# Written order of issue carried into the second product of an attention and channel-mixer kernel

## The chip, the core and the metric

One core of a Trainium2 chip runs the kernel. The metric is the device time of one execution in microseconds (us). The core has a matmul engine (PE, with its weight loads as PEld), a vector engine (DVE), a scalar engine (ACT), a general engine (POOL) and an engine that issues most transfers (SP). Each has its own queue of instructions, worked off in order; semaphores tie them together.

## The reference

Attention with a decay per head, in blocks, gives x of shape (4, 768, 512). A low-rank mixer along the sequence and a channel mixer of two products follow:

```python
xt = x.transpose(0, 2, 1)
h = xt @ U @ V
u = x + h.transpose(0, 2, 1)
ch = np.maximum(u @ w_ch1, 0.0) @ w_ch2
return (u + ch).astype(np.float32)
```

`u` has 3072 rows of 512 numbers, `w_ch1` is 512 x 2048, `w_ch2` is 2048 x 512.

## The kernel before

All products are made at fp32 accuracy from numbers split in three: high, low, and a third part that corrects both. One full product of two tiles is then two "high" matmuls (high and low of one operand) on one PSUM bank and one "third" matmul on another, or on the same bank once ACT has scaled it (`raise_high`, L966).

The first product, r = u @ w_ch1, is cut in `g`, six groups of 512 rows of u, and `ft`, 16 blocks of 128 columns of w_ch1. Groups 0 to 3 are plain (`hidden`, `single`); groups 4 and 5 come last and use seven products in place of eight for most pairs of blocks: `seven_of` (L1213) for j = 1 to 7, `eight_of` (L1264) for j = 0. These products take sums of parts of u, the **forms** (a11, a12, s1 to s4 and so on), made by `form` (L1103): a `high` on ACT (L1109), `rest` (L1112) and `last` (L1115) on DVE, each 128 x 1024. Each r tile (128 x 512) goes to memory (`r_d`).

The order of this part is written by hand, inside `tc.manual_schedule()` (`ordered`, L811 to L1409). `sequence` (L1070) lists its 53 products; `tick()` (L1173) is called once in each of them, between its high matmuls and what follows, and runs the steps that `strew` (L1045) has put at that number: loads and splits of weights, forms, stores. A tick is some 1.4 us, in j = 0 some 2.7 us. The last pair, j = 7, ends with `(7, 3)`, `(7, 6)` on the running banks z and d, and `(7, 7)` on the same two. `taken` (L1198) copies a bank to an r tile on ACT (L1200), `add_to` (L1195) adds another on DVE (L1196), `give` (L1203) stores the tile two ticks later, or at once when fewer than two are left.

The second product, ch = relu(r) @ w_ch2, runs over 96 steps (g, ft), ft within g. A step loads an r tile (`fetch`, L1302, three buffers), takes its relu and splits it into m (`split`, L1307: L1311 on ACT, L1312 and L1313 on DVE; four buffers) and makes four pieces of three matmuls (`product`, L1318: L1327, L1329, L1331). `ahead(i)` (L1360) loads step i + 3 and splits step i + 2. A piece has two PSUM banks for the 16 steps of its group; pieces 0 and 1 of group 0 take tags b1 and b2, pieces 2 and 3 take a1 and a2. After step 15 of a group `finish` (L1341) adds u, loaded by `residual` (L1333, L1339), and stores.

The 16 blocks of w_ch2 are split in three as well (`w2_split`, L1369, by `divided_steps`, L255). Five (`EARLY`) are done in ticks of the first product. The other eleven are divided in the loop of the second: in step i the load of block i + 5 (L1381), then L266 on ACT, L267 and L270 on DVE. Their places are those of the forms, which the first product no longer needs.

From L1409 on, the order in which instructions are put in the queues is chosen by the planner of the language: it goes by its own costs, and puts an instruction that it finds ready in front of written ones that it finds waiting. The first steps of the second product are thus mixed into the end of the first.

```python
    ordered.close()
    spare = 1
    STAG = 3
    for i in range(len(steps) - STAG):
        g, ft = steps[i]
        ahead(i)
        if i + EARLY < FT:
            for step in w2_split(i + EARLY):
                step()
```

Of the kernel before, what the change touches and what calls it, by code (L numbers as in the profile page):

```python
# [9 lines left out]
F32R = mybir.dt.float32r  # L10
# [4 lines left out]
P = 128  # L15
# [3 lines left out]
def kernel(  # L19
# [28 lines left out]
    nc = tc.nc  # L48
# [4 lines left out]
    C = H * D  # L53
    CT = C // P
    FF = moe_w_ch1.shape[1]
    FT = FF // P
# [6 lines left out]
    TG = N // P  # L63
# [10 lines left out]
    hl_pool = ctx.enter_context(tc.tile_pool(name="hl", bufs=FG))  # L74
    d_pool = ctx.enter_context(tc.tile_pool(name="d", bufs=FG))
# [28 lines left out]
    w2_d = [dram.tile([P, C], FP32, name=f"w2_d{ft}") for ft in range(FT)]  # L104
    forms_d = [dram.tile([P, 8, C // 2], FP32, name=f"forms_d{j}") for j in range(FT // 2)]

    def tmp(name):
        return wconv.tile([P, C], FP32, tag="tmp", bufs=2, name=name)
# [100 lines left out]
    def plain(keep, key, tag="wf"):  # L209

        def dst():
            if key not in keep:
                keep[key] = (
                    tmp("wg") if tag == "tmp" else
                    plain_pool[-1].tile(
                        [P, C], FP32, tag=tag, bufs=1 if len(plain_pool) == 1 else 3, name="wf"
                    )
                )
            return keep[key]

        return dst
# [33 lines left out]
    def divided_steps(parts, fetch, engine, apart=False, raw=None):  # L255

        st = {}

        def load():
            st["w"] = raw() if raw and apart else plain({}, 0)()  # L260
            fetch(st["w"])

        def split():
            hi, low, third = parts()
            w = st["w"][:, 0 : hi.shape[-1]]
            nc.scalar.mul(hi, w, E * NEAR)  # L266
            nc.vector.scalar_tensor_tensor(  # L267
                low, hi.bitcast(FP32), -1.0 / E, w, ALU.mult, ALU.add
            )
            engine.tensor_tensor(  # L270
                out=third, in0=low.bitcast(FP32), in1=hi.bitcast(FP32), op=ALU.subtract
            )

        def high():
            st["hi"], st["low"], st["third"] = parts()
            nc.scalar.mul(st["hi"], st["w"][:, 0 : st["hi"].shape[-1]], E * NEAR)

        def low():
            nc.vector.scalar_tensor_tensor(  # L279
                st["low"], st["hi"].bitcast(FP32), -1.0 / E,  # L280
                st["w"][:, 0 : st["hi"].shape[-1]], ALU.mult, ALU.add,
            )

        def third():
            engine.tensor_tensor(  # L285
                out=st["third"], in0=st["low"].bitcast(FP32), in1=st["hi"].bitcast(FP32),
                op=ALU.subtract,
            )

        return [load, high, low, third] if apart else [load, split]  # L290

    more_w = []
# [31 lines left out]
    raw = {}  # L324

    def parts(s):
        return 2 if s == 0 else 1
# [65 lines left out]
    st = {}  # L393
# [305 lines left out]
    for s in range(NS):  # L699
# [6 lines left out]
        step = [("fade", s)] * (c > 0)  # L706
# [104 lines left out]
    ordered = ctx.enter_context(ExitStack())  # L811
# [55 lines left out]
    def banks(n, other):  # L867

        tags = ("b1", "b2") if other else ("a1", "a2")
        pzs, pds = ([bank([P, N], name, tag) for i in range(n)] for name, tag in zip(("pz", "pd"), tags))  # L870
        return list(zip(pzs, pds))
# [56 lines left out]
    places = (0, 5), (1, 8), (1, 9), (1, 20), (1, 21), (1, 23), (2, 7), (2, 8)  # L928
# [19 lines left out]
    LAST, EARLY = FT - 4, 5  # L948
# [96 lines left out]
    def strew(units, steps):  # L1045
        assert len(units) == len(steps)
        for n, step in zip(units, steps):
            at.setdefault(n, []).append((units[0], step))
# [21 lines left out]
    sequence = []  # L1070
# [10 lines left out]
    for n in range(0, len(sequence), 2):  # L1081
# [6 lines left out]
        def fetch(w, n=n):  # L1088
            for i, (j, form) in enumerate(sequence[n : n + 2]):
                nc.sync.dma_start(out=w[:, i * HC : (i + 1) * HC], in_=forms_d[j][:, form])  # L1090
# [5 lines left out]
    places, form_of = {}, {}  # L1096

    def place(n):
        hl = hl_pool.tile([P, 2, CT, N], F32R, tag="hl", name="s_hl")
        d = d_pool.tile([P, CT, N], F32R, tag="d", name="s_d")  # L1100
        places[n] = [(hl[:, :, c : c + 2], d[:, c : c + 2]) for c in range(0, CT, 2)]

    def form(key, n, i, of):  # L1103

        hl, d = form_of[key] = places[n][i]
        hi, low = hl[:, 0], hl[:, 1]

        def high():
            nc.scalar.mul(hi, of, NEAR)  # L1109

        def rest():
            nc.vector.tensor_tensor(out=low, in0=of, in1=hi.bitcast(FP32), op=ALU.subtract)  # L1112

        def last():
            nc.vector.scalar_tensor_tensor(  # L1115
                d, hi.bitcast(FP32), E, low.bitcast(FP32), ALU.mult, ALU.subtract
            )

        return [high, rest, last]

    def sums(out, a, b, op=ALU.subtract):
        return [lambda: nc.vector.tensor_tensor(out=out, in0=a, in1=b, op=op)]

    g0, g1 = range(FG, NG)
    a11, a12, a21, a22 = (whole[g][:, c : c + 2] for g in (g0, g1) for c in (0, 2))
    s12 = sums_pool.tile([P, 2, 2, N], FP32, tag="s", bufs=1, name="s")
    s1, s2 = s12[:, 0], s12[:, 1]
    s3 = s12[:, 0]
# [31 lines left out]
    def last_forms():  # L1160
        place(3)
        strew((0,), sums(s3, a11, a21))
        strew((0, 1, 1), form("s4", 3, 0, a12))
        strew((1, 2, 2), form("s3", 3, 1, s3))
        strew((3,), [forms_made])

    def forms_made():
        whole_ctx.close()
# [29 lines left out]
    def taken(acc, scale):  # L1198
        t = r_pool.tile([P, N], FP32, tag="r", name="r")
        nc.scalar.mul(t, acc, scale)  # L1200
        return t

    def give(t, ft, g):  # L1203
        n = at["now"] + 2
        step = lambda: nc.sync.dma_start(out=r_d[ft][g], in_=t)
        strew((n,), [step]) if n < len(sequence) else step()

    def both(z, d):
        t = taken(z, 4096.0 + 1.0)
# [89 lines left out]
    steps = [(g, ft) for g in range(NG) for ft in range(FT)]  # L1299
    rs, ms = {}, {}  # L1300
# [6 lines left out]
    def split(i):  # L1307
        r = rs.pop(i)
        ms[i] = m = m_pool.tile([P, 3, N], F32R, tag="m", name="m")
        hi, low = m[:, 0].bitcast(FP32), m[:, 1].bitcast(FP32)  # L1310
        nc.scalar.activation(out=m[:, 0], in_=r, func=AF.Relu, scale=NEAR)  # L1311
        nc.vector.scalar_tensor_tensor(m[:, 1], r, 0.0, hi, ALU.max, ALU.subtract)  # L1312
        nc.vector.scalar_tensor_tensor(m[:, 2], hi, E, low, ALU.mult, ALU.subtract)  # L1313
# [4 lines left out]
    def product(i, n, parts=range(3)):  # L1318
        g, ft = steps[i]
        m, (hi, low, third) = ms[i], w2t[ft]  # L1320
        if ft == 0:
            acc[n] = banks(1, n // 2 != spare)[0]
        pz, pd = acc[n]
        cols = slice(n * P, (n + 1) * P)
        first, end = ft == 0, ft == FT - 1
        if 0 in parts:
            nc.tensor.matmul(out=pz, lhsT=m[:, 0, cols], rhs=hi, start=first, stop=False)  # L1327
        if 1 in parts:
            nc.tensor.matmul(out=pz, lhsT=m[:, 1, cols], rhs=low, start=False, stop=end)  # L1329
        if 2 in parts:  # L1330
            nc.tensor.matmul(out=pd, lhsT=m[:, 2, cols], rhs=third, start=first, stop=end)  # L1331
# [28 lines left out]
    def ahead(i):  # L1360
        if i + 3 < len(steps):
            fetch(i + 3)
        if i + 2 < len(steps):
            split(i + 2)


    w2t = {}

    def w2_split(ft):  # L1369
        def raw():  # L1370
            t = e_pool[0].tile([P, 3, C], F32R, tag="e", name="w2")
            w2t[ft] = [t[:, i, :] for i in range(3)]
            return w2t[ft][2].bitcast(FP32)

        if ft >= EARLY and (ft - EARLY) % 4 == 0:
            hl = hl_pool.tile([P, 4, 2, C], F32R, tag="hl", name="w2_hl")
            d = d_pool.tile([P, 4, C], F32R, tag="d", name="w2_d")
            for i in range(min(4, FT - ft)):
                w2t[ft + i] = [hl[:, i, 0], hl[:, i, 1], d[:, i]]
        return divided_steps(  # L1380
            lambda: w2t[ft], lambda w: nc.sync.dma_start(out=w, in_=w2_d[ft]),  # L1381
            nc.gpsimd if ft < EARLY else nc.vector,
            ft < EARLY, raw,
        )

    def begin_second():
# [7 lines left out]
    total = len(sequence)  # L1394
    strew((total - 14,), [begin_second])
    for ft in range(EARLY):
        n = 6 + 7 * ft
# [2 lines left out]
        strew((total - 9 + n,), [lambda n=n: fetch(n)])  # L1400
    for n in range(2):
        strew((total - 4 + 2 * n,), [lambda n=n: split(n)])
    pending = []
    for j in range(FT // 2):
        (seven_of if j in SEVEN else eight_of)(j, pending)
    for end in pending:
        end()
    assert list(at) == ["now"]
    ordered.close()  # L1409
    spare = 1  # L1410

    STAG = 3
    for i in range(len(steps) - STAG):
        g, ft = steps[i]
        ahead(i)
        if i + EARLY < FT:
            for step in w2_split(i + EARLY):
                step()
        if i == len(steps) - STAG - 1:
            ahead(i + 1)  # L1420
        if ft == FT - STAG - 1:
            residual(g)
        for n in range(TG):
            product(i, n)
        del ms[i]
        if ft == FT - 1:
            for n in range(TG):
                finish(g, n)
# [36 lines left out]
```

## Time and profile before

| what | value |
|---|---|
| three runs | 643.47, 643.88 (median), 645.03 us |
| the profiled execution | 643.46 us, of it a span of 641.6 us from the first to the last instruction |
| PE busy | 632.1 us, 99% of the span |
| DVE, ACT, POOL busy | 464.5, 331.9, 147.8 us |
| mean granted PE clock | 0.996 of full speed |
| matmuls from 300 to 350, 350 to 400 us | 220, 204 |
| last matmul of the first product starts | between 377.0 and 377.6 us |

In a row of the timeline the columns are start, duration, engine, line, operation, tiles written and read, how often; where several are merged, the duration runs from the first start to the last end. A bracket is idle time of that engine before the row, with what ended it. "Matmuls are pipelined": the end of one lies after the start of the next. In a table by stage each row is a stretch, with the busy time of each engine and the count of its instructions, then the granted clock, the share of the transfer engines and GB/s.

### The profile page before, as it was taken

What the parts mean: (1) busy time and instruction counts of PE and PEld (TensorE: products, weight loads), DVE (VectorE), ACT (ScalarE), POOL (GpSimd) and SP (SyncE); (2) the same over time, 40 slices, a digit from 0 to 9 for tenths busy, and PEclk for the clock granted to TensorE, in tenths of its full rate; (3) what the DMA queues carried; (4) which work ended last, traced back from release to release, by engine and by line L of the source; (5) the groups of instructions that cost most, each with busy time, mean ns of one, the idle gap of its engine ahead of it and who ended that gap; (6) DMA issues with size and microseconds to landing.
All of it is one profiled execution on the core that took longest, in us unless ns stands there. A gap on an engine that the chain in (4) does not pass through costs nothing.

```text
span 641.6 us, 13618 instructions
## 1 busy us (share of the span) xinstructions
PE 632.1 (99%) x5200; PEld 530.3 (83%) x5200; DVE 464.5 (72%) x738; ACT 331.9 (52%) x607; POOL 147.8 (23%) x124
## 2 busy tenths in 40 slices
PE   8999999999999999999999999999999999999997
PEld 7988989788888888887887768888888888888886
DVE  6765878657878889779698899685575755855854
ACT  4775865646777777777776644232322322323320
POOL 4475978000000000000567600030120300300300
PEclk9999999999999999999999989999999999999999
DMA  9989995458987888665667786362363363543521
GB/s 234 254 202 256 256 231 146 139 192 289 317 300 276 285 307 287 222 203 176 211 214 229 253 314 219 97 228 101 98 230 98 116 202 100 174 147 99 181 83 65
DMA packets 141379, 128.83 MB, mean 201 GB/s; under 512 B 82498, under 2 KB 99394, under 8 KB 141314
## 3 DMA queue, kind: packets, MB, share of 16 engines
q1 hardware_dynamic: 116192, 121.53, 59.0%
q10 hardware_dynamic: 25122, 6.42, 4.4%
q8 instruction: 41, 0.67, 0.4%
q14 instruction: 24, 0.20, 0.1%
HBM read 78.64 MB, written 48.89 MB: 199 GB/s over the span
## 4 chain that ended last, share of the span: by engine, by line
PE 94%; ACT 2%; DMA 2%; SPq 1%; issue 1%; DVE 0%; ACTq 0%; DVEq 0%
PE pz L959 25%; PE pz L1327 14%; PE pz L1329 14%; PE pd L1331 13%; PE px L514 4%; PE z L959 4%; PE pss L463 3%; PE p L959 3%; PE pz L889 2%; PE px L525 2%; PE d L959 2%; PE pqk L416 2%; PE pkv L486 1%; PE c L959 1%; PE pd L900 1%; PE pm L618 1%
## 5 line engine op out<-in xcount | busy, mean ns | idle before, releaser
L1311 ACT ACTIVATE m<-rm 128x512 fp32r<-128x512 f32 x96 | 60.5, 631 | 176.7 <-PE pd L1331 145.8
L1312 DVE SCALAR_TENSOR_TENSOR m<-rm,m 128x512 fp32r<-128x512 f32 x96 | 71.9, 750 | 84.7 <-ACT m L1311 84.7
L959 PE MATMUL pz<-u_hl,w 128*128 128x512 f32 x448 | 110.3, 389 | 0.0
L1327 PE MATMUL pz<-w_hl,m 128*128 128x512 f32 x264 | 102.7, 389 | 0.0
L1329 PE MATMUL pz<-w_hl,m 128*128 128x512 f32 x264 | 102.7, 389 | 0.0
L1331 PE MATMUL pd<-w_d,m 128*128 128x512 f32 x264 | 101.4, 389 | 0.0
L959 PEld LDWEIGHTS pz<-u_hl,w 128*128 128x128 f32 x448 | 84.1, 188 | 17.4
L285 POOL TENSOR_TENSOR w<-w 128x512 fp32r<-128x512 f32 (+1 forms) x28 | 41.6, 1510 | 215.0 <-DVE w L279 202.4
L1313 DVE SCALAR_TENSOR_TENSOR m<-m 128x512 fp32r<-128x512 f32 x96 | 75.2, 783 | 2.7
L1356 POOL TENSOR_TENSOR o<-o,u 128x512 f32<-128x512 f32 x20 | 29.8, 1518 | 200.6 <-DVE o L1352 200.6
L959 PE MATMUL pz<-u_d,w 128*128 128x512 f32 x224 | 59.7, 389 | 0.0
L1331 PEld LDWEIGHTS pd<-w_d,m 128*128 128x128 f32 x264 | 49.6, 188 | 10.4
L1327 PEld LDWEIGHTS pz<-w_hl,m 128*128 128x128 f32 x264 | 49.6, 188 | 10.2
L1329 PEld LDWEIGHTS pz<-w_hl,m 128*128 128x128 f32 x264 | 49.6, 188 | 10.2
L959 PEld LDWEIGHTS pz<-u_d,w 128*128 128x128 f32 x224 | 42.0, 188 | 8.8
L966 ACT ACTIVATE pz<-pz 128x512 f32<-128x512 f32 x60 | 34.9, 581 | 27.3 <-PE pz L959 27.3
L1329 PE MATMUL pz<-w,m 128*128 128x512 f32 x120 | 47.2, 393 | 0.0
L1327 PE MATMUL pz<-w,m 128*128 128x512 f32 x120 | 47.0, 393 | 0.0
L1331 PE MATMUL pd<-w,m 128*128 128x512 f32 x120 | 46.8, 391 | 0.0
L472 DVE TENSOR_TENSOR sm<-pss,mask 128x512 f32<-128x512 f32 x48 | 30.9, 685 | 16.9 <-PE pss L463 16.9
L970 ACT ACTIVATE r<-pz 128x512 f32<-128x512 f32 x60 | 35.7, 596 | 14.3 <-PE pz L959 13.1
L196 DVE SCALAR_TENSOR_TENSOR sc<-words,sc 128x512 uint32<-128x512 uint32 (+2 forms) x34 | 24.3, 713 | 21.2 <-ACT sc L178 21.2
(143 smaller groups left out, 1114.2 us busy)
## 6 DMA issues: line engine op xcount, KB each, us to landing
r_d<-r SPq DMA_DIRECT2D x96, 256.0 KB, 2.8
rm<-r_d SPq DMA_DIRECT2D x96, 256.0 KB, 2.6
words<-in_moe_w_ch_dram SPq DMA_DIRECT2D x30, 512.0 KB, 4.6
wf<-forms_d SPq DMA_DIRECT2D x53, 128.0 KB, 2.8
u_d<-x_nat SPq DMA_DIRECT2D x24, 256.0 KB, 3.9
u<-u_d SPq DMA_DIRECT2D x24, 256.0 KB, 4.2
qraw<-in_q_dram SPq DMA_DIRECT2D x23, 256.0 KB, 4.9
out_dram<-o SPq DMA_DIRECT2D x23, 256.0 KB, 2.0
```

What stands on the lines that cost most here:

```text
L285: engine.tensor_tensor(out=st["third"], in0=st["low"].bitcast(FP32), in1=st["hi"].bitcast(FP32), op=ALU.subtract,)
L472: nc.vector.tensor_tensor(out=sm[:, x], in0=pss[:, x], in1=mask[:, x], op=ALU.mult)
L959: nc.tensor.matmul(out=out, lhsT=weights, rhs=moving, start=start and i == 0, stop=i == len(pieces) - 1, skip_group_check=not start,)
L966: nc.scalar.mul(acc, acc, 1.0 + E)
L970: nc.scalar.mul(r, acc, 4096.0)
L1311: nc.scalar.activation(out=m[:, 0], in_=r, func=AF.Relu, scale=NEAR)
L1312: nc.vector.scalar_tensor_tensor(m[:, 1], r, 0.0, hi, ALU.max, ALU.subtract)
L1313: nc.vector.scalar_tensor_tensor(m[:, 2], hi, E, low, ALU.mult, ALU.subtract)
L1327: nc.tensor.matmul(out=pz, lhsT=m[:, 0, cols], rhs=hi, start=first, stop=False)
L1329: nc.tensor.matmul(out=pz, lhsT=m[:, 1, cols], rhs=low, start=False, stop=end)
L1331: nc.tensor.matmul(out=pd, lhsT=m[:, 2, cols], rhs=third, start=first, stop=end)
L1356: nc.gpsimd.tensor_tensor(out=o, in0=o, in1=u, op=ALU.add)
```

## The change

The `ordered` region now takes in the first eleven steps of the second product, in a loop of its own, and the planner starts with step 11. In a step the loop issues, in this order: the load of r for step i + 3, the load of block i + 7 of w_ch2, up to two of the stores that are left over, the matmuls, the split of r for step i + 2, and the high, low and third of block i + 5. The division of the eleven blocks is cut in these single steps (L276, L279, L285, on the same engines as before), and the loads of the first two of them stand at ticks 51 and 52. In step 0 the pieces run in the order 0, 2, 1, 3.

`give` no longer stores at once when fewer than two ticks are left: those three stores are kept in `last_gives` and issued in steps 1 and 2, behind the loads of these steps.

The making of two forms goes a tick, or a sum, later: s4 from ticks 0, 1, 1 to 1, 2, 2 and s3 from 1, 2, 2 to 2, 3, 4; the sum that s3 comes from stays at tick 0.

```diff
-            st["w"] = raw() if raw and apart else plain({}, 0)()
+            st["w"] = raw() if raw else plain({}, 0)()
...
-        strew((0, 1, 1), form("s4", 3, 0, a12))
-        strew((1, 2, 2), form("s3", 3, 1, s3))
-        strew((3,), [forms_made])
+        strew((1, 2, 2), form("s4", 3, 0, a12))
+        strew((2, 3, 4), form("s3", 3, 1, s3))
+        strew((4,), [forms_made])
...
+    last_gives = []
+
     def give(t, ft, g):
         n = at["now"] + 2
         step = lambda: nc.sync.dma_start(out=r_d[ft][g], in_=t)
-        strew((n,), [step]) if n < len(sequence) else step()
+        if n < len(sequence):
+            strew((n,), [step])
+        else:
+            last_gives.append(step)
...
-        if ft >= EARLY and (ft - EARLY) % 4 == 0:
-            hl = hl_pool.tile([P, 4, 2, C], F32R, tag="hl", name="w2_hl")
-            d = d_pool.tile([P, 4, C], F32R, tag="d", name="w2_d")
-            for i in range(min(4, FT - ft)):
-                w2t[ft + i] = [hl[:, i, 0], hl[:, i, 1], d[:, i]]
+        def places():
+            if ft not in w2t:
+                hl = hl_pool.tile([P, 4, 2, C], F32R, tag="hl", name="w2_hl")
+                d = d_pool.tile([P, 4, C], F32R, tag="d", name="w2_d")
+                for i in range(min(4, FT - ft)):
+                    w2t[ft + i] = [hl[:, i, 0], hl[:, i, 1], d[:, i]]
+            return w2t[ft]
+
         return divided_steps(
-            lambda: w2t[ft], lambda w: nc.sync.dma_start(out=w, in_=w2_d[ft]),
-            nc.gpsimd if ft < EARLY else nc.vector,
-            ft < EARLY, raw,
+            places, lambda w: nc.sync.dma_start(out=w, in_=w2_d[ft]),
+            nc.gpsimd if ft < EARLY else nc.vector, True, early if ft < EARLY else None,
         )
...
+    w2_late = [w2_split(ft) for ft in range(EARLY, FT)]
+    for n in range(2):
+        strew((total - 2 + n,), w2_late[n][:1])
...
+    for i in range(FT - EARLY):
+        fetch(i + 3)
+        if i + 2 < FT - EARLY:
+            w2_late[i + 2][0]()
+        if i:
+            for step in last_gives[:2]:
+                step()
+            del last_gives[:2]
+        for n in (0, 2, 1, 3) if i == 0 else range(TG):
+            product(i, n)
+        del ms[i]
+        split(i + 2)
+        for step in w2_late[i][1:]:
+            step()
+    assert not last_gives
     ordered.close()
-    for i in range(len(steps) - STAG):
+    for i in range(FT - EARLY, len(steps) - STAG):
         g, ft = steps[i]
         ahead(i)
-        if i + EARLY < FT:
-            for step in w2_split(i + EARLY):
-                step()
```

More of the change, by code (lines that the diff above doesn't have):

```diff
@@ L1369, in w2_split, with early @@
     def w2_split(ft):
-        def raw():
+        def early():
             t = e_pool[0].tile([P, 3, C], F32R, tag="e", name="w2")
@@ L1408 @@
     assert list(at) == ["now"]
-    ordered.close()
     spare = 1
     STAG = 3
-    for i in range(len(steps) - STAG):
+    for i in range(FT - EARLY):
[13 more added lines that the diff above has]
+    assert not last_gives
+    ordered.close()
+    for i in range(FT - EARLY, len(steps) - STAG):
         g, ft = steps[i]
         ahead(i)
-        if i + EARLY < FT:
-            for step in w2_split(i + EARLY):
-                step()
         if i == len(steps) - STAG - 1:
```

## The prediction

> **What bounds the kernel.** I read the page's busy shares first, then the table by stage, then matmuls in order of time around every stage that falls short, then the waits there.
>
> ```profile
> PE 632.1 (99%) x5200; PEld 530.3 (83%) x5200; DVE 464.5 (72%) x738; ACT 331.9 (52%) x607; POOL 147.8 (23%) x124
> ```
>
> PE sets the end, so time can only come from places where matmuls do not follow each other at their own pace. That pace is 0.227 us: from 361.90 to 369.64 us there are 34 matmuls, 7.74 / 34. By it 100 us of this part hold 440 matmuls, and the table by stage gives 440 from 200 to 300 and 220 from 300 to 350, but only 204 from 350 to 400, where 220 fit; from 400 to 600 it is full again. So one place matters, the passage from the first product to the second:
>
> ```profile
> core 0: us, PE busy (x) PEld busy (x) DVE busy (x) ACT busy (x) POOL busy (x), PEclk, DMA share, GB/s
> 360.00:369.64 9.64, 9.64 (x43) 7.66 (x42) 7.33 (x11) 5.48 (x11) 6.24 (x5) 1.00 0.88 282
> 369.64:373.41 3.77, 2.40 (x9) 1.16 (x7) 3.13 (x6) 3.35 (x7) 0.00 (x0) 1.00 0.95 346
> 373.41:377.63 4.22, 4.22 (x12) 3.35 (x12) 3.87 (x7) 2.11 (x4) 0.00 (x0) 0.60 0.81 275
> 377.63:382.00 4.37, 4.37 (x21) 3.59 (x20) 3.94 (x7) 0.63 (x1) 0.00 (x0) 1.00 0.95 345
> ```
>
> Two kinds of loss stand in it: waits in the second row, a granted clock of 0.60 in the third. PE in order of time:
>
> ```profile
> 369.64 1.07 PE L959 MATMUL z<-s_hl,w 128*128 128x512 f32 x4
> 370.61 0.70 PE L959 MATMUL d<-s_d,w 128*128 128x512 f32 x2
> 371.87 0.73 PE L959 MATMUL p<-s_d,w 128*128 128x512 f32 x2 [0.56 <-ACT p L966]
> 373.41 1.66 PE L959 MATMUL z<-s_hl,w 128*128 128x512 f32 x4 [0.81 <-ACT r L1200]
> ...
> 377.63 0.40 PE L1331 MATMUL pd<-w,m 128*128 128x512 f32 x1
> ```
>
> From 369.64 to 377.63 PE starts 19 matmuls (4+2+2+4, five of the second product, 2): at its pace 4.31 us, in fact 7.99, a loss of 3.68. The first eight should end at 371.45 and the ninth started at 373.41: 1.96 us of waits. The other eleven took 4.22 where 2.49 were due: 1.73 us of slow clock. Why ACT is late is on ACT's own row:
>
> ```profile
> 367.68 0.59 ACT L1200 ACTIVATE r<-z 128x512 f32<-128x512 f32 x1
> 370.04 1.29 ACT L266 ACTIVATE w_hl<-wf 128x512 fp32r<-128x512 f32 x2 [1.77 <-DMA wf<-w_d]
> 371.23 0.58 ACT L966 ACTIVATE p<-p 128x512 f32<-128x512 f32 x1
> 371.75 1.13 ACT L1311 ACTIVATE m<-rm 128x512 fp32r<-128x512 f32 x2
> 372.79 0.57 ACT L1200 ACTIVATE r<-z 128x512 f32<-128x512 f32 x1
> ```
>
> L266 is a w2 division of the second product. The planner has put two of them ahead of L966, and the first waits for a load issued at 365.04 (chain of waits: 4.98 us). L966 could have begun at about 369.04: its matmuls, the four `p` of 367.83, end at 368.90, and ACT begins 0.14 after such an end elsewhere (366.47 + 1.07 to 367.68). It ran 2.2 us late.
>
> A second, smaller loss is at the start of the Strassen-like products:
>
> ```profile
> 295.33 1.97 PE L959 MATMUL pz<-s_hl,w 128*128 128x512 f32 x8
> 297.67 1.21 PE L959 MATMUL pz<-s_d,w 128*128 128x512 f32 x4 [0.37 <-ACT pz L966]
> 298.72 2.01 PE L959 MATMUL pz<-s_hl,w 128*128 128x512 f32 x8
> ```
>
> Twelve matmuls from 295.33 should bring the next to 298.05; it came at 298.72: 0.67 lost. ACT had the `high` of form s4 (L1109, 296.08, 1.05 us) ahead of that L966 (297.03).
>
> **The forms.** The high of s4 goes from tick 0 to tick 1, s3 and the closing of its buffers follow. L966 of tick 0 then runs at 296.08 to 296.68, ahead of the third pieces at 297.15. In tick 1 ACT has L276 (0.62), L1109 (1.05) and L966 (0.58): done at about 298.9, wanted after the second high, 299.87. The instructions on DVE stay the same (two L1112, two L1115 at 1.22), now behind those of the weights; s3 is ready at about 304.6, as in the trace, and is read about 7 us later, so the shift costs nothing. Gain 0.67 less a restart; I take 0.6.
>
> **The written order.** No instruction is added or dropped: the eleven w2 divisions were L266, L267, L270 (625, 689, 688 ns) and become L276, L279, L285 (629, 686, 692 by the rows of that shape on ACT and DVE): nothing. They are moved behind the end of the first product. So ACT has, after L1200 at 367.68: L966 369.04 to 369.62, L1311 of step 1 to 370.2, then L1200 of `z` as soon as that is summed (369.64 + 1.07 + 0.14 = 370.85, to 371.43). PE has its four matmuls in between (two `d`, two `p`) until 371.60, so neither wait remains.
>
> What is late next is DVE. Its row has L1313 of step 0 at 368.75 (1.11, beside POOL) and the sum c12 + d at 369.78, which already holds the `d` of 370.61 by 0.14 in all and will still do so. Then, at 0.60 from start to start as DVE's row shows from 374.20 on: c11 370.4, L1312 and L1313 of step 1 at 371.0 and 371.6, and c22 + d at 372.2, done at 372.9. The last `d` matmuls overwrite nothing but add on the same bank, so they wait for it: due 372.5, they start at 372.95, with a restart of 0.08. The second product starts at 373.46, where 14 matmuls at full pace from 369.64 would give 372.82. Loss 0.64 instead of 3.68: gain 3.04.
>
> The order 0, 2, 1, 3 of step 0: piece 1 takes the banks of `three` and `five`, free after the last of three more sums at 374.66; as third in line it starts at 374.82. As second it would wait 0.5. Covered, by 0.16.
>
> Then eleven steps of 12 matmuls, 2.72 us each. DVE has four operations in each, 2.41 us. It reaches step 2's split at 375.2 and ends it at 376.5; PE needs it at 378.9. The lead of 2.4 us grows by 0.3 a step. ACT has two operations, 1.2 us. The w2 forms are ready some 9 us before use. If POOL ran beside DVE (L1313 averages 783 ns over the kernel), four would take 3.1 and the lead would be gone in six steps; POOL has no operation from 370 to 400.
>
> SP: each step has a load of r (0.32 us to issue) and one of w2 (0.32), whose buffer is free only after the L279 three steps before. Behind that blocked load stands the next load of r. From that L279 to the one three steps on: 0.7 for two issues, the landing, 0.8 for L1311, 1.9 for three operations of DVE, in all the landing plus 3.4. In three steps PE takes 8.16, so landings up to 4.8 us are hidden. The trace has 4.0 (r) and 3.7 (w2) as medians from 360 to 392, and 2.6 for r over the kernel. The seven u loads that the planner already puts here (L1339, 0.42 us of SP each) can fall between again; if three come in a row, SP loses 1.3 us, less than the lead. The three stores moved behind the loads free buffers that nobody takes before the outputs of step 15, some 40 us later: nothing.
>
> **Sum.** 0.6 + 3.04 = 3.6 us. The profiled execution took 643.46 (span 641.6, 1.9 around it): 639.9. It is the fastest shown, 0.4 below the median of 643.88, so the forecast is 640.2. All waits gone would be 4.35, 639.5.
>
> **Rivals.** (1) The clock falls all the same: a gain of only 3.6 - 1.73, 642.0. For it: I have only two rows of the bound, waits of 0.67 in 4 us that left the clock at 1.00 (294 to 298) and 1.96 in 3.77 that were followed by 0.60; the 0.64 that I leave is near the first. [...] (2) The seam only moves: the planner takes over at step 11 and the same 3.7 us are lost there, 643.5 to 643.9, no change. Against it: nothing of step 11 or later waits for a late w2 load or stands ahead of a PE release, and the present stretch of planned steps, 400 to 600, loses nothing. This also covers an order that comes out as before. (3) A few waits of PE for r or DVE beyond the lead, 1 to 2 us: 641.2 to 642.2. (4) Slower: the ring through SP. With landings of 6.5 us one round takes 9.9 against 8.16; three rounds lose 5.2, less the lead of 2.4, 2.8; waits like these bring the slow clock, twice 1.73. Together 6.3 against the gain of 3.6: 646.6. It decides against the change from about 6 us; the longest landing of r in the whole kernel is 5.5, so it needs u loads, stores and loads piled up.
>
> **Chances.** Forecast 0.62, (1) 0.12, (2) 0.08, (3) 0.08, (4) 0.10. The range takes in the forecast, (1) and (3), 0.82: 639.3 to 642.6. Against 643.88 a change under 0.3%, 1.9 us, cannot be told from none, so the border is 641.95: faster 0.62 + 0.08 + half of (1), 0.76; same 0.14; slower 0.10.
>
> **What would show it.** Right: no L276 of w2 ahead of the last L966; granted clock 1.00 all through; about 219 matmuls from 350 to 400; the last `d` waiting about 0.4 for DVE L1196; the first L1327 near 372.9 (0.6 earlier than the above, by the forms); no wait at 297.67. Wrong: a stretch below 1.00, PE waiting for L1313 or L285 between steps 2 and 11, or L1305 blocked on SP until its L1311 is late.

## The result, and the profile after

The changed kernel takes 642.54 us (median of 22 executions, 639.69 to 644.60) against 644.00 (22 executions, 642.31 to 648.67) before. The ratio is 0.9963, with a 95% interval of 0.9947 to 0.9979: about 2.4 us faster, 1.4 to 3.4. The two medians alone lie 1.5 us apart. The forecast was 640.2, in a range of 639.3 to 642.6; the median lies 0.06 us inside its upper end.

The profiled execution is the quickest of the 22: 639.69 us with a span of 637.9, which is 3.7 less than in the profile before (641.6). The forecast for the profiled execution was 639.9, and 0.2 us is closer than its grounds allow: the fronts of two executions of one kernel can differ by 6 us (run again, below), and those of these two happen to differ by 0.3. The typical execution gained less, and most of what follows is about that difference.

In the changed kernel the lines of the second product are five further on: L1311, L1312, L1313 are L1316, L1317, L1318, and L1327, L1329, L1331 are L1332, L1334, L1336. The loads of r are L1310, those of w2 L1389, those of u L1344.

The passage by stage, same columns as before:

```profile
369.00:373.00 4.00, 3.55 (x16) 2.41 (x15) 3.86 (x7) 1.91 (x5) 0.00 (x0) 1.00 0.87 286
373.00:377.00 4.00, 4.00 (x19) 3.31 (x18) 3.93 (x7) 2.68 (x5) 0.00 (x0) 1.00 0.95 337
377.00:382.00 5.00, 5.00 (x24) 4.14 (x23) 4.86 (x9) 0.24 (x2) 0.00 (x0) 1.00 0.98 310
```

None of these stretches has a clock below 1.00, and PE stands still for 0.45 us only. Its matmuls in order of time:

```profile
368.71 1.07 PE L959 MATMUL z<-s_hl,w 128*128 128x512 f32 x4
369.70 0.70 PE L959 MATMUL d<-s_d,w 128*128 128x512 f32 x2
370.23 0.62 PE L959 MATMUL p<-s_d,w 128*128 128x512 f32 x2
370.69 1.08 PE L959 MATMUL z<-s_hl,w 128*128 128x512 f32 x4
372.22 0.70 PE L959 MATMUL d<-s_d,w 128*128 128x512 f32 x2 [0.45 <-DVE r L1196]
372.76 0.40 PE L1332 MATMUL pz<-w,m 128*128 128x512 f32 x1
```

From the first `z` the twentieth matmul starts at 373.92, after 5.21 us; before it was 7.99. The third `p` and the last `z` wait no more; the last `d` waits for DVE's sum, as forecast. ACT shows why:

```profile
366.75 0.59 ACT L1200 ACTIVATE r<-z 128x512 f32<-128x512 f32 x1
368.00 0.58 ACT L966 ACTIVATE p<-p 128x512 f32<-128x512 f32 x1 [0.66 <-PE p L959]
368.49 0.62 ACT L1316 ACTIVATE m<-rm 128x512 fp32r<-128x512 f32 x1
369.81 0.60 ACT L1200 ACTIVATE r<-z 128x512 f32<-128x512 f32 x1 [0.69 <-PE z L959]
```

L966 waits for PE, no longer for a load, and it starts 0.71 us before the first `z` of the passage, where it started 1.59 us after it. At the start of j = 0 the matmuls now follow each other without a wait, 295.15, 296.97 and 297.87:

```profile
295.15 1.98 PE L959 MATMUL pz<-s_hl,w 128*128 128x512 f32 x8
296.97 1.07 PE L959 MATMUL pz<-s_d,w 128*128 128x512 f32 x4
297.87 1.98 PE L959 MATMUL pz<-s_hl,w 128*128 128x512 f32 x8
```

### The profile page after: what moved, and what is told of

Read it like the earlier page. It is cut to its first block, busy times and chain, and to the rows that moved or that the text cites. A ratio compares the mean times of both kernels' runs of the same rounds, so it can differ in the third digit from the quotient of the medians.

```text
span 637.9 us, 13619 instructions
## 1 busy us (share of the span) xinstructions
PE 629.9 (99%) x5200; PEld 529.8 (83%) x5200; DVE 465.3 (73%) x738; ACT 331.4 (52%) x607; POOL 148.0 (23%) x124
## 4 chain that ended last, share of the span: by engine, by line
PE 95%; ACT 2%; DMA 1%; issue 1%; DVE 1%; ACTq 0%; POOL 0%; DVEq 0%; SPq 0%; POOLq 0%
PE pz L959 26%; PE pz L1334 14%; PE pz L1332 14%; PE pd L1336 14%; PE z L959 4%; PE pss L463 4%; PE px L514 3%; PE p L959 3%; PE pz L889 2%; PE d L959 2%; PE px L525 2%; PE pqk L416 2%; PE c L959 1%; PE pkv L486 1%; PE pd L900 1%; PE pm L618 1%
## 5 line engine op out<-in xcount | busy, mean ns | idle before, releaser
L1316 ACT ACTIVATE m<-rm 128x512 fp32r<-128x512 f32 x96 | 60.6, 632 | 174.7 <-PE pd L1336 134.6
L1317 DVE SCALAR_TENSOR_TENSOR m<-rm,m 128x512 fp32r<-128x512 f32 x96 | 71.8, 749 | 80.8 <-ACT m L1316 80.8
L1332 PE MATMUL pz<-w_hl,m 128*128 128x512 f32 x264 | 102.7, 389 | 0.0
L1334 PE MATMUL pz<-w_hl,m 128*128 128x512 f32 x264 | 102.7, 389 | 0.0
L1336 PE MATMUL pd<-w_d,m 128*128 128x512 f32 x264 | 101.4, 389 | 0.0
L285 POOL TENSOR_TENSOR w<-w 128x512 fp32r<-128x512 f32 (+1 forms) x28 | 41.6, 1508 | 214.3 <-DVE w L279 201.7
L1318 DVE SCALAR_TENSOR_TENSOR m<-m 128x512 fp32r<-128x512 f32 x96 | 75.3, 784 | 3.0
L1334 PEld LDWEIGHTS pz<-w_hl,m 128*128 128x128 f32 x264 | 49.5, 188 | 10.4
L1332 PEld LDWEIGHTS pz<-w_hl,m 128*128 128x128 f32 x264 | 49.5, 188 | 10.3
L1336 PEld LDWEIGHTS pd<-w_d,m 128*128 128x128 f32 x264 | 49.6, 188 | 10.2
L966 ACT ACTIVATE pz<-pz 128x512 f32<-128x512 f32 x60 | 34.9, 581 | 27.2 <-PE pz L959 27.1
L1334 PE MATMUL pz<-w,m 128*128 128x512 f32 x120 | 46.7, 389 | 0.0
L1332 PE MATMUL pz<-w,m 128*128 128x512 f32 x120 | 46.7, 389 | 0.0
L1336 PE MATMUL pd<-w,m 128*128 128x512 f32 x120 | 46.7, 389 | 0.0
```

Of the source, the lines that this page charges most:

```text
L285: engine.tensor_tensor(out=st["third"], in0=st["low"].bitcast(FP32), in1=st["hi"].bitcast(FP32), op=ALU.subtract,)
L966: nc.scalar.mul(acc, acc, 1.0 + E)
```

## The experiments

Theory: PE lost time at two places, at the start of j = 0 (the form ahead of L966) and in the passage (planned ACT instructions ahead of L966 and L1200, and a slow clock after the waits); the written order takes both away. This is theory A of the texts below. Rivals: the planner's mixture is not the cause; the first profile of the changed kernel was a lucky one (B); the slow clock has another cause.

One measure is used throughout: the time from the last group of `z` but one (368.71 above) to the end of the span, called the last part. It leaves out all that came before, which differs by several us between executions of one kernel. It is 271.96 us in the profile before and 269.2 in the one after.

**The changed kernel again.** No edit.

> The changed kernel once more, unaltered. Theory A: the time went out of the passage between the products and out of the start of the Strassen-like products, in every execution alike; then the 19 matmuls of the passage take 5.2 us again (8.0 before), no wait at the start of j = 0, and the span differs from 637.9 only by what the front of the kernel (first 100 us, paced by loads) adds. Rival B: the first profile was a lucky execution, and in others PE waits for r or DVE in steps 2 to 11; then the matmuls from 372 to 402 us fall short of 132 and L1316 or L1318 is named as the releaser.

644.72 us beside 646.57 of the kernel before on that chip, ratio 0.9944 (0.9919 to 0.9969). The span of the profile is 644.1, 6.2 more than the first time, but the last part takes 269.2 us again, with the same wait of 0.45. The 6.2 us are lost in the front: the first matmul of L889 starts at 118.0 us, at 111.9 in the first profile. PE's waits show 4 of the 6 (engine, line, what it waited for: us in all, times, longest):

```profile
PE pm L618 <- DMA vp<-vp: 2.2, 2, 1.8
PE pss L463 <- issue: 2.0, 1, 2.0
```

In the first profile these were 0.2 us and none. Theory A holds, rival B falls: the passage is the same, and what varies is the front, which both kernels have.

**The two forms alone**, in the kernel before:

```diff
-        strew((0, 1, 1), form("s4", 3, 0, a12))
-        strew((1, 2, 2), form("s3", 3, 1, s3))
-        strew((3,), [forms_made])
+        strew((1, 2, 2), form("s4", 3, 0, a12))
+        strew((2, 3, 4), form("s3", 3, 1, s3))
+        strew((4,), [forms_made])
```

> The kernel before with only the two forms a sum later. Theory A: the wait of 0.67 us at the start of j = 0 goes, the passage stays at 8.0 us with a granted clock near 0.60 in its second half, so 0.6 us faster than before (0.1%, less than the times can tell; read from the matmuls). Rival C: the planner answers with another order at the seam, and the passage moves by a microsecond or more.

Ratio 1.0010 (0.9981 to 1.0039): nothing that the time can tell, as 0.1% should be. The wait at j = 0 is gone from the profile. The surprise is in the passage:

```profile
375.75 1.07 PE L959 MATMUL z<-s_hl,w 128*128 128x512 f32 x4
376.74 0.70 PE L959 MATMUL d<-s_d,w 128*128 128x512 f32 x2
378.06 0.73 PE L959 MATMUL p<-s_d,w 128*128 128x512 f32 x2 [0.61 <-ACT p L966]
379.61 1.19 PE L959 MATMUL z<-s_hl,w 128*128 128x512 f32 x4 [0.82 <-ACT r L1200]
380.64 0.39 PE L1327 MATMUL pz<-w,m 128*128 128x512 f32 x1
```

The waits are those of the kernel before (0.61 and 0.82 beside 0.56 and 0.81), but the matmuls after them run at 0.23 us: the clock did not fall. The 19 matmuls took 6.48 us, not 7.99. So neither the theory's 8.0 nor rival C: the matmuls stand in the same order as before, the waits recur, and the slow clock comes only sometimes.

**The written order alone**: the changed kernel with the three lines above undone.

> The changed kernel with the two forms where they were. Theory A: passage 5.2 us, clock 1.00, but 0.67 us lost at the start of j = 0: 0.6 us slower than the changed kernel, 3.0 faster than before. Rival: the wait at j = 0 is absorbed by other slack, no difference to the changed kernel.

644.29 us, ratio 0.9940 (0.9908 to 0.9973). The passage is that of the changed kernel (last part 269.2, wait of `d` 0.45), and j = 0 loses 0.65: the eight matmuls that start at 300.50 should bring the next at 302.31,

```profile
302.84 1.19 PE L959 MATMUL pz<-s_d,w 128*128 128x512 f32 x4 [0.37 <-ACT pz L966]
303.87 2.00 PE L959 MATMUL pz<-s_hl,w 128*128 128x512 f32 x8
```

and with the four after them the next is due at 303.22. The gain in time is that of the written order; the forms add 0.65 to 0.7, seen in PE's rows alone.

**The kernel before again.** No edit.

> The kernel before, unaltered, for a second look at its passage. Theory A with D: the waits are those of the first profile (about 2 us, behind L966 and L1200), since the order of the instructions is fixed; the slow clock after them comes in about half of the executions, so the 19 matmuls take 6.4 to 6.5 us without it and up to 8.0 with it. Rival: waits and clock go together, and the passage takes 8.0 us in every execution of this kernel.

```profile
375.03 0.73 PE L959 MATMUL p<-s_d,w 128*128 128x512 f32 x2 [0.17 <-ACT p L966]
376.58 1.20 PE L959 MATMUL z<-s_hl,w 128*128 128x512 f32 x4 [0.82 <-ACT r L1200]
377.62 0.39 PE L1327 MATMUL pz<-w,m 128*128 128x512 f32 x1
```

The first wait is shorter this time, the clock is 1.00, and the 19 matmuls take 6.06 us, 1.75 more than at full pace. Three executions with the planner's order thus took 7.99, 6.48 and 6.06; three with the written order (changed, again, order) 5.2 each. The rival falls. Without the slow clock the written order is worth 0.9 to 1.3 us, with it 2.8.

**A wait made by hand.** In the changed kernel, 5, 7 or 12 needless copies on ACT ahead of the last L966:

```diff
+    def hold():
+        t = r_pool.tile([P, N], FP32, tag="r", name="r")
+        for i in range(7):
+            nc.scalar.mul(t, ms[0][:, 0].bitcast(FP32), 1.0)
+
+    strew((total - 3,), [hold])
```

> The changed kernel with seven needless ACT copies (0.52 us apart) put ahead of the last L966, at tick 50; they read the m of step 0 and write a tile that nobody reads. A wait of known size, with no load and no planner in it. Theory A: PE waits as it did before, about 2.4 us in two pieces (third p, then z), the wait of d for DVE goes, so the 18 matmuls from the first z to the fourth of the second product take 6.6 us in place of 5.0. Theory D, on the clock: waits of some 2 us spread over 4 us make the granted clock fall in a part of the executions, by the phase at which they fall; then about half of the executions of this kernel have a mean clock under 0.998, as those of the kernel before have (17 of 32), and few of the changed one (6 of 34); an execution with the fall is 1 to 2 us longer. [...]

> As with seven needless ACT copies ahead of the last L966, but five of them. Theory A: seven made the third p wait 2.03 us, 0.52 a copy, so five make it wait 1.0; z and d follow with 0.3 to 0.5 each. Theory D: the share of executions with a mean clock under 0.998 lies between that of the changed kernel (6 of 34) and that with seven (8 of 12). [...]

> As before, with twelve copies. Theory A: the third p waits 4.6 us. Theory D: nearly every execution has a mean clock under 0.998, and is longer than the changed kernel by 3.8 us of waits and 1 to 2 us of slow clock. [...]

With seven:

```profile
376.66 0.74 PE L959 MATMUL p<-s_d,w 128*128 128x512 f32 x2 [1.97 <-ACT p L966]
377.69 1.24 PE L959 MATMUL z<-s_hl,w 128*128 128x512 f32 x4 [0.29 <-ACT r L1200]
379.35 1.19 PE L959 MATMUL d<-s_d,w 128*128 128x512 f32 x2 [0.42 <-DVE r L1196]
380.34 0.63 PE L1332 MATMUL pz<-w,m 128*128 128x512 f32 x1
380.77 0.63 PE L1334 MATMUL pz<-w,m 128*128 128x512 f32 x1
```

From 380.34 to 380.77 a matmul takes 0.43 us, where 0.23 is full pace (granted clock 0.94 from 370 to 380 us, 0.89 from 380 to 390): the slow clock of the kernel before, made with no planner and no load. By the starts of the matmuls the third `p` comes 1.0 us late with five copies (forecast 1.0), 2.3 with seven and 5.6 with twelve (forecast 4.6); by the profile's count of idle time 0.64, 1.97 and 5.29. A copy costs 0.66 us (from the last group of `z` but one to the third `p` are 3.66 us with seven copies and 6.97 with twelve), not the 0.52 of the expectations. `d` still waits for DVE with five and seven copies, which the expectation for seven had not. With seven the 18 matmuls take 9.05 us, where 6.6 were expected without a slow clock, and with twelve the last part is 7.2 us longer than in the changed kernel, where 4.8 to 5.8 were expected.

| kernel | ratio to before | executions with a mean clock under 0.998 |
|---|---|---|
| before, all executions beside experiments | 1 | 45 of 84 |
| forms alone, planner's order | 1.0010 (0.9981 to 1.0039) | 7 of 12 |
| changed | 0.9963 and 0.9944 | 6 of 34 |
| order, split1, best, last_split (all with the written order) | 0.9940 to 0.9978 | 8 of 45 |
| changed, 5 copies | 0.9971 (0.9950 to 0.9991) | 1 of 12 |
| changed, 7 copies | 1.0009 (0.9981 to 1.0036) | 8 of 12 |
| changed, 12 copies | 1.0063 (1.0039 to 1.0088) | 12 of 12 |

An ACT instruction ahead of L966 is enough to give back the whole gain: seven copies, and the kernel is as slow as before. The counts of the table take in the whole execution, not the passage alone: the profiles with seven and twelve copies have a slow stretch in the front too, with a mean granted clock of 0.99 over the first 120 us, where five copies had 1.00. On the clock the course with longer waits is as theory D has it from five to twelve, but five copies are too few by its own account: they lost 2.4 us in three pieces (18 matmuls in 6.50 us, where 4.08 are due), no less than the 2.2 of the forms kernel in two, and the clock fell in 1 of 12, against 7 of 12 there. So it is not the sum of the waits that decides.

Nor does the fall need one long wait: in the profile with seven copies no wait of PE is over 2.0 us, and in the passage of the kernel before none is over 0.81. How close the waits lie does not decide alone either. In the kernel before four matmuls start in the 2.80 us from 370.61 to 373.41, and from 373.41 to 377.63 the granted clock is 0.60. In the forms kernel four start in the 2.87 us from 376.74 to 379.61, with the waits in the same two places, and the clock stays at 1.00. What decides is not shown by these runs.

**The split of step 1 behind more sums.**

```diff
-        strew((total - 4 + 2 * n,), [lambda n=n: split(n)])
+        strew((total - 4 + 3 * n,), [lambda n=n: split(n)])
```

> The changed kernel with the split of r for step 1 at tick 52 in place of 51. Theory A: the last two d matmuls wait 0.45 us for the sum c22 + d, because the two DVE operations of that split stand ahead of it; behind the sums they cost nothing, since step 1 begins 2.7 us after step 0: the wait goes, the 19 matmuls take 4.6 us in place of 5.2. Rival: the split of step 1 is then late itself, PE waits for L1318 at the start of step 1, or the last piece of step 0 waits for its bank, and nothing is gained.

The theory's half is right, and the rival's too. `d` follows at once, but the last piece of step 0 now waits for its bank, whose sum stands behind the split:

```profile
376.84 0.39 PE L1334 MATMUL pz<-w,m 128*128 128x512 f32 x1
377.65 0.50 PE L1336 MATMUL pd<-w,m 128*128 128x512 f32 x1 [0.42 <-DVE r L1196]
```

A wait of 0.45 us has gone, one of 0.42 has come. Last part 269.2, as in the changed kernel; ratio 0.9952 (0.9922 to 0.9982).

**The splits of steps 0 and 1 earlier, and DVE's operations between each other.**

```diff
-        strew((total - 9 + n,), [lambda n=n: fetch(n)])
+        strew((total - 13 + n,), [lambda n=n: fetch(n)])
...
-        strew((total - 4 + 2 * n,), [lambda n=n: split(n)])
+        strew((total - 6 + 2 * n,), [lambda n=n: split(n)])
...
-        split(i + 2)
-        for step in w2_late[i][1:]:
-            step()
+        split(i + 2, w2_late[i][1:])
```

(`split` then issues ACT's L276 after its own ACT operation, L279 between its two DVE operations and L285 behind them, in the order L1317, L279, L1318, L285.)

> The changed kernel with two edits: the first three loads of r at ticks 40 to 42 and the splits of steps 0 and 1 at ticks 47 and 49 (44 to 46, 49 and 51); and in the eleven steps the three operations of a w2 block put between the two DVE operations of the split. Theory A: with one split less among the last sums, neither d nor the last piece of step 0 waits for L1196; the 18 matmuls take 4.1 to 4.3 us in place of 5.0, no wait in step 0, 0.7 faster than the changed kernel (not to be told by the times alone). Theory E: on DVE an operation that reads what the one just before it wrote starts 0.72 us after it, one that does not 0.60; put between each other, four operations take 2.4 us a step in place of 2.66. Rival: the splits that come earlier make the sums of j = 6 late, and PE waits there instead; DVE's step stays at 2.66, set by something else.

Theory A fails. The early splits fall beside POOL, which is busy from 366.80 to 370.12; there DVE's operations take up to 1.68 us for 0.68. The second split stands ahead of the sum c12 + d, and the last `d` but one now waits 1.70 us for that sum (in this kernel L1319 and L1322 are DVE's two operations of a split):

```profile
368.99 1.68 DVE L1322 SCALAR_TENSOR_TENSOR m<-m 128x512 fp32r<-128x512 f32 x1
370.59 0.68 DVE L1196 SCALAR_TENSOR_TENSOR r<-d,r 128x512 f32<-128x512 f32 x1
371.19 0.41 DVE L279 SCALAR_TENSOR_TENSOR w<-w,wf 128x256 fp32r<-128x256 f32 x1
371.52 0.68 DVE L1319 SCALAR_TENSOR_TENSOR m<-rm,m 128x512 fp32r<-128x512 f32 x1
372.24 1.10 DVE L1322 SCALAR_TENSOR_TENSOR m<-m 128x512 fp32r<-128x512 f32 x1
373.26 0.68 DVE L1196 SCALAR_TENSOR_TENSOR r<-d,r 128x512 f32<-128x512 f32 x1
```

Last part 270.3, 1.1 more than in the changed kernel; ratio 0.9978 (0.9952 to 1.0004). Theory E holds: one step of DVE is 2.40 us,

```profile
378.08 0.68 DVE L1319 SCALAR_TENSOR_TENSOR m<-rm,m 128x512 fp32r<-128x512 f32 x1
378.68 0.68 DVE L279 SCALAR_TENSOR_TENSOR w_hl<-w_hl,wf 128x512 fp32r<-128x512 f32 x1
379.28 0.69 DVE L1322 SCALAR_TENSOR_TENSOR m<-m 128x512 fp32r<-128x512 f32 x1
379.88 0.69 DVE L285 TENSOR_TENSOR w_d<-w_hl 128x512 fp32r<-128x512 f32 x1
380.48 0.68 DVE L1319 SCALAR_TENSOR_TENSOR m<-rm,m 128x512 fp32r<-128x512 f32 x1
```

and 2.66 in the changed kernel (first split at 374.58, next at 377.24):

```profile
374.58 0.68 DVE L1317 SCALAR_TENSOR_TENSOR m<-rm,m 128x512 fp32r<-128x512 f32 x1
375.30 0.69 DVE L1318 SCALAR_TENSOR_TENSOR m<-m 128x512 fp32r<-128x512 f32 x1
375.91 0.68 DVE L279 SCALAR_TENSOR_TENSOR w_hl<-w_hl,wf 128x512 fp32r<-128x512 f32 x1
376.63 0.69 DVE L285 TENSOR_TENSOR w_d<-w_hl 128x512 fp32r<-128x512 f32 x1
377.24 0.69 DVE L1317 SCALAR_TENSOR_TENSOR m<-rm,m 128x512 fp32r<-128x512 f32 x1
```

L1318 reads what L1317 wrote and starts 0.72 after it; L279 reads nothing of L1318 and starts 0.61 after it.

**The split of step 1 behind all sums**, with the same order in steps 1 to 10:

```diff
-    for n in range(2):
-        strew((total - 4 + 2 * n,), [lambda n=n: split(n)])
+    strew((total - 4,), [lambda: split(0)])
...
     assert list(at) == ["now"]
+    split(1)
     spare = 1
```

> The changed kernel with the split of r for step 1 behind the last sum (in place of tick 51), and in steps 1 to 10 the operations of a w2 block between the two DVE operations of the split. Theory A: all five sums stand ahead of it, so neither d nor the last piece of step 0 waits for L1196; the split ends 0.2 us before step 1 reads it; from the first z to the end of step 0 (26 matmuls) 6.1 us in place of 6.8, 0.7 faster than the changed kernel, and DVE takes 2.41 us a step. Rival: with the split of step 1 last, those of steps 2 and 3 have a lead of 0.6 us where they had 2.2, and any late load of r shows as a wait of PE for L1316 or L1318 in steps 1 to 4, 0.5 us or more.

As forecast: PE has no wait from the passage on, the 18 matmuls take 4.26 us (4.98 in the changed kernel), and the last part 268.5, 0.7 less than in the changed kernel.

```profile
374.86 1.08 PE L959 MATMUL z<-s_hl,w 128*128 128x512 f32 x4
375.78 0.62 PE L959 MATMUL d<-s_d,w 128*128 128x512 f32 x2
376.23 0.39 PE L1338 MATMUL pz<-w,m 128*128 128x512 f32 x1
```

ACT waited for loads of r eight times from 365 to 400 us, 3.3 us at most, and none of it reached PE. 641.73 us beside 646.40, ratio 0.9942 (0.9910 to 0.9974). It beats the kernel before; that it beats the changed kernel is seen in PE's rows, and the times are too coarse to show it.

**The pieces of step 0 in the order 0, 1, 2, 3.**

> The changed kernel with the pieces of step 0 in the order 0, 1, 2, 3. Theory A: piece 1 waits for the bank that the last of the three sums p frees: 0.6 us more between the first and the fourth piece, then nothing. Rival: the banks are free by then, no wait.

The wait comes, but it is half as long: the 12 matmuls of step 0 take 3.08 us (374.68 to 377.76) for 2.76, so 0.3 us, not 0.6. Two short waits, before the pz and the pd of piece 1, make it up.

**The last three stores ahead of the loads.**

```diff
-            last_gives.append(step)
+            step()
```

> The changed kernel with the last three stores of r issued where they were, ahead of the loads of steps 3 and 4. Theory A: SP is held until the last sum; the load of step 3 is issued some 4 us later (375 in place of 370.6), its split on DVE comes 1 to 2 us later, PE does not wait, since it has a lead of 2 us: no change of the passage or the steps. Rival: the ring through SP runs late from then on and PE waits for L1318 in steps 3 to 6, 1 us or more, perhaps with a fall of the clock.

The rival came true. SP is held by six loads of u (3.23 us from 373.60 on) and then by the stores at 378.61 and 380.08, which wait for the last sums, and the load of r for step 3 leaves at 381.10, 7.3 us after the first `z` of the passage, where it left 1.9 us after it in the changed kernel. It lands late, and step 3 comes to a stop at each of its operands in turn:

```profile
385.82 0.39 PE L1336 MATMUL pd<-w,m 128*128 128x512 f32 x1
386.56 0.50 PE L1332 MATMUL pz<-w,m 128*128 128x512 f32 x1 [0.35 <-ACT m L1316]
387.29 0.50 PE L1334 MATMUL pz<-w,m 128*128 128x512 f32 x1 [0.22 <-DVE m L1317]
388.01 0.51 PE L1336 MATMUL pd<-w,m 128*128 128x512 f32 x1 [0.22 <-DVE m L1318]
388.35 0.40 PE L1332 MATMUL pz<-w,m 128*128 128x512 f32 x1
```

2.53 us for four matmuls that take 0.91: 1.6 lost. The last part takes 271.3, 2.1 more than in the changed kernel. By this one profile, the written order with the stores in their old place would give back most of what it gains.

## Why the prediction was right, and where it was not

- **Where the time was.** Both places were right, and so was the cause: an ACT instruction ahead of L966. The forms lost 0.67 us before and nothing after (forms, order), where 0.6 was forecast. Of the signs that were named, the order on ACT, the clock of 1.00 up to the last matmul, the wait of the last `d` (0.45), the first L1332 at 372.76 and the start of j = 0 all came; 216 matmuls stand between 350 and 400 us, where 219 were named.
- **The size of the passage.** Forecast gain 3.04, measured between the two profiles 7.99 - 5.21 = 2.78. The remaining loss is 0.90 in place of 0.64: L1318 starts 0.71 after L1317, not the 0.60 that was read from rows of operations that do not depend on each other, and the matmuls need a little longer to follow each other again (the last two `d` 0.54 us to the next start, 372.22 to 372.76, where 0.45 is their pace).
- **The term that was mis-sized: 1.73 us of slow clock.** It was read from one execution and counted as if in all. Of three profiles with the planner's order one has it, and 45 of 84 executions of the kernel before have a mean clock under 0.998, against 6 of 34 of the changed kernel, which has no slow stretch in its passage in either profile. If the difference (54 less 18 in a hundred) falls to the passage, the slow clock is worth 0.36 x 1.7, some 0.6 us, on the mean. With 0.9 to 1.3 for the waits and 0.7 for the forms this makes 2.2 to 2.6, beside the measured 2.4. This is an estimate, and one figure speaks for more: executions with a mean clock under 0.998 are some 3 us longer by their medians in the kernel before (648.4 beside 645.7 us, 647.0 beside 643.8, 647.3 beside 644.2), not 1.7; where the rest is lost is open. That the 18 in a hundred come from the front is likely: two profiles of other kernels, with seven and with twelve copies, show a fall there (0.99 over the first 120 us), and the two profiles of the changed kernel show none in its passage (1.00).
- **The time forecast**, 640.2, was 2.3 us low. The slow clock is 1.1 of this, by the estimate above, and the size of the passage 0.3; the rest is the 0.9 by which the ratio and the medians differ, and it stays unexplained. That the range held, by 0.06 us, is luck: the sum counted a loss of some executions as if it were in all, and the upper end stood for a rival. Rival (1) has the right time, 642.0, for another reason: it is not that the clock falls all the same after the change, but that it did not always fall before.
- **Rivals (2) and (3)** did not occur: PE's list of waits in the profile after names none behind the last `d`, neither in steps 2 to 11 nor later, though ACT waited for a load of r up to 4.8 us.
- **Rival (4), the ring through SP**, was rightly seen as the danger, and it shows when the stores are put back. But the three stores were priced at nothing, by the buffers that they free; what they would cost ahead of the loads was not counted. In the change it costs nothing; undone it costs 1.6 to 2.1 us.
- **The lead of DVE** was right at its start (2.2 us measured: the split of step 2 ends at 375.99, step 2 begins at 378.2), but it does not grow by 0.3 a step: DVE's step is 2.66 us, not 2.41. The planner's mixture before had given DVE the better order.
- **The order 0, 2, 1, 3** was said to save 0.5; it saves 0.3.

## What to carry to other kernels

Where an engine with its queue in order holds work that another waits for, look at what the planner has put ahead of it. In a written order, count every transfer that stands behind a waiting store. A loss read from one execution has parts that recur and parts that do not: take a second profile of the same kernel before pricing the slow clock. When executions differ by more than the effect, measure from a landmark late in the kernel to its end.

## What the hardware showed that was not expected

- The granted clock was 0.60 from 373.41 to 377.63 us, behind two waits of PE below 1 us each (0.56 and 0.81), in one of three profiles with the planner's order. Behind 0.61 and 0.82, and behind 0.17 and 0.82, it was 1.00.
- Two DVE operations of 0.69 us started 0.60 to 0.61 us apart, but 0.71 to 0.72 when the second reads what the first wrote. With an independent operation between them four took 2.40 us in place of 2.66.
- The front of this kernel, the first 120 us, cost 6 us more in one execution than in another, with the same program.
